# A fourth token tile read transposed, and two weight splits moved, in a linear-attention and gated-FFN kernel

## The chip, the core and the metric

The kernel runs on one core of one Trainium2 chip. The metric is the device time of one execution in microseconds; the median of three runs is given, with the lowest and the highest. One execution was also taken by the hardware profiler. The engines are named as the profile names them: PE (TensorE matmuls), PEld (TensorE weight loads), DVE (VectorE), ACT (ScalarE), POOL (GpSimd) and SP (SyncE, which issues all DMAs here).

## The reference

x has 2048 tokens of 576 features. It is layer-normalized once; the normalized x feeds a linear attention (32 heads of 18) and a feed-forward network of width 4608, whose output gates that of the attention.

```python
def _A_ref(x, wqkv, wo):                       # linear attention
    q, k, v = ...(x @ wqkv)                    # 32 heads of 18
    phi = lambda t: jnp.where(t > 0, t + 1, jnp.exp(t)) + 1e-6
    pq, pk = phi(q), phi(k)
    kv = jnp.einsum("bhsd,bhse->bhde", pk, v)
    z = jnp.einsum("bhsd->bhd", pk)
    num = jnp.einsum("bhqd,bhde->bhqe", pq, kv)
    den = jnp.einsum("bhqd,bhd->bhq", pq, z)[..., None] + 1e-6
    return (num / den ...) @ wo

def _B_ref(x, w1, b1, w2, b2):                 # feed-forward
    h = _gelu(jnp.einsum("bsd,df->bsf", x, w1) + b1)
    return jnp.einsum("bsf,fd->bsd", h, w2) + b2

xn = _layernorm(x, axis=-1)
s = _A_ref(xn, A_wqkv, A_wo)
g = _silu(_B_ref(xn, B_w1, B_b1, B_w2, B_b2))
return x + s * g
```

## The kernel before, in words

All arrays are float32. A matmul takes float32r operands, so each operand is split into a high part (a cast on ACT) and a low part (the difference, mostly on DVE), and a product is the sum of high by high, high by low and low by high. The work has three stages.

**Stage 1, keys and values** (the loop at line 539, one pass for each of 16 token tiles of 128). In pass t, TensorE projects tile t to keys (`pk`, 28 matmuls at line 313), adds the state product of tile t-1 (`ps_kva`, `ps_kvb`, line 382) and projects tile t to values (`pv`, line 313). The projection needs the normalized x of the tile transposed, features on partitions, as `xh` and `xl`. There are two ways to it, and `NTR` (line 41) says how many tiles take the first:

- tiles below NTR: x comes in rows (`load_x`); `statistics` (lines 187 to 196: bn_stats on DVE, a power on POOL) gives mean and reciprocal deviation; `normalize_x` (ACT, line 221, with `offset` on DVE before it) normalizes; `transpose_x` makes five transposes on TensorE (line 232) and takes the result out of PSUM into `xh` (ACT, line 238) and `xl` (DVE, lines 246 and 247).
- tiles from NTR on: x comes already transposed from a second input xT (`load_xt`, line 255). There the mean and deviation of each token lie along the free dimension, so `store_stats` (line 260) writes the two numbers of each token to DRAM and `load_stats` (line 264) reads them back into all 128 partitions (`bc`). `center` (POOL, line 276) subtracts, `scale` (DVE, line 279) multiplies, `set_x_hi` (ACT, line 287) and `set_x_lo` (DVE, lines 291 and 292) split. TensorE does nothing for them.

In pass t the code makes tile t+1 ready. Between these steps the pass prepares operands of the feed-forward weights: `w2_load`, `w2_sum` (POOL, 405), `w2_hi`, `w2_lo`, `w2_store` (`w2r`, `w2o`), and `we_load`, `we_sums` (POOL, 440), `we_hi` (ACT, 446), `we_lo` (DVE, 450), `we_store` (`w1u`, `w1h`). The tiles `xt` (which `xn` shares) and `bc` have three buffers each; the `xh` and `xl` of tiles 12 to 15 take the place of `w1h` and `w1u`.

**Stage 2, queries and attention** (the loop at line 1070).

**Stage 3, feed-forward** (the loop at line 1512). 18 steps: 9 chunks of four 128-wide feature blocks, for two halves of the tokens. In a step, two pairs of blocks (j = 0 and 1) go through `Up.step` seven times each (`UP`, line 1454): products at line 1148 into the banks `a`, `b`, `zy` and `e`, which DVE combines (lines 1168, 1171, 1174, 1181, 1185) and ACT turns into gelu values `g` (line 1156). Bank `e` is written twice by a pair: by step 5, whose result DVE reads at line 1174, and by step 3, which adds to what stands there. Then come seven products with w2 (`product`, line 1287). The last step is plain: it has no such products; the four blocks of w2 are split at `set_hi` (813) and `set_lo` (816) as `w__11202`, `w__11213`, `w__11226` and `w__11301`, and `down_plain` (line 1403) multiplies with them.

What each step does beside the products stands in a table written by hand: `add(base + n, fn)` puts fn behind the n-th of 28 places of a step (0 to 6 are the first pair, 7 to 13 the second), and `at_step` runs it. In stages 1 and 2 every engine, in stage 3 every engine but SP, executes in the order in which the code emits (`in_order`, line 59). DMAs are all issued by SP.

Of the kernel before, what the change touches and what calls it, by code (L numbers as in the profile page):

```python
# [22 lines left out]
NT = S // P  # L23
# [14 lines left out]
NGT = 8  # L38
NWARM = 20

NTR = 4


@with_exitstack
def linear_attention_gated_ffn(ctx, tc, x, xT, wqkv, wo, w1, w1e, b1, w2, b2, out):
# [129 lines left out]
    def load_x(t):  # L175
        xraw[t] = (
            stw.tile([P, D], F32, tag="stw", name=f"x{t}") if t < 2 else stage(D, f"x{t}")
        )
        for cs in (slice(0, HD), slice(HD, D)) if t == 0 else (slice(0, D),):
            nc.sync.dma_start(xraw[t][:, cs], x[t * P : (t + 1) * P, cs])  # L180
# [3 lines left out]
    def xt_tile(name):  # L184
        return t1.tile([P, KT * P], F32, tag="xt", name=name, bufs=3)

    def statistics(t):

        st = t1.tile([P, 2, 6], F32, tag="st", name=f"st{t}")
        nc.vector.bn_stats(st[:, 0, :], xraw[t][:, :HD])  # L190
        nc.vector.bn_stats(st[:, 1, :], xraw[t][:, HD:])
        mv = t1.tile([P, 4], F32, tag="mv", name=f"mv{t}", bufs=4)
        nc.vector.bn_aggr(mv[:, 0:2], st)
        nc.vector.tensor_scalar_add(mv[:, 2:3], mv[:, 1:2], 1e-5)
        nc.gpsimd.tensor_tensor(mv[:, 1:2], mv[:, 2:3], nhalf, op=ALU.pow)
        stats[t] = mv

    def layernorm(t):
        statistics(t)
        if t == 0:  # L200
            mv = stats[t]
            xn[t] = xt_tile(f"xn{t}")
            for dst, src in norm_parts(t):
                nc.vector.tensor_scalar(dst, src, mv[:, 0:1], mv[:, 1:2], op0=SUB, op1=MUL)
# [8 lines left out]
    def norm_parts(t):  # L213
        return (xn[t][:, :D], xraw[t]), (xn[t][:, D:], xraw[t][:, 512:])
# [40 lines left out]
    def load_xt(t):  # L255
        raw = xt_tile(f"xt{t}")
        xts[t] = raw.rearrange("p (k c) -> p k c", k=KT)
        nc.sync.dma_start(raw, xT[t])
# [5 lines left out]
    def load_stats(t):  # L264
        bcs[t] = t1.tile([P, P, 2], F32, tag="bc", name=f"bc{t}", bufs=3)
        src = st_dram[t]
        nc.sync.dma_start(
            bcs[t].rearrange("p c v -> p (c v)"),
            bass.AP(tensor=src.tensor, offset=src.offset, ap=[[0, P], [1, 2 * P]]),
        )  # L270

    def of_tokens(t, v):
        return bcs[t][:, None, :, v].to_broadcast([P, KT, P])

    def center(t):
        nc.gpsimd.tensor_tensor(xts[t], xts[t], of_tokens(t, 0), op=SUB)
# [152 lines left out]
    def we_load(q):  # L429
        if not we:  # L430
            we["u"] = x_lo(3, "w1u").rearrange("p a b -> p (a b)").bitcast(F32)
            we["h"] = x_hi(3, "w1h").rearrange("p a b -> p (a b)")
        u = we["u"][:, (q % 2) * 1024 : (q % 2) * 1024 + 1024]
        we[q] = u.rearrange("p (b c) -> p b c", b=8)
        nc.sync.dma_start(u[:, :512], w1e[q])
# [103 lines left out]
    for t in range(NT):  # L539
        for n in {0: (3, 4, 5), 1: (6, 7), 2: (8, 9)}.get(t, (t + 7,)):  # L540
            if n < NT:
                load_x(n)
        if t == 1:
            we_load(0), we_load(1)
        for n in (NTR, NTR + 1) if t == 2 else (t + 3,) if t > 2 else ():
            if n < NT:
                load_xt(n)
                load_stats(n)
        if 0 < t < NTR - 2:
            layernorm(t + 2)  # L550
        for n in {0: (), 1: (4, 5), 2: (6, 7)}.get(t, (t + 5,)):
            if n < NT:
                statistics(n)
                store_stats(n)
        if NTR <= t + 2 < NT:
            center(t + 2)
        if NTR <= t + 1 < NT:
            scale(t + 1)
        pk = bank2(f"pk{t}")
        v_t = v_bufs[t % 2]  # L560
        sums2 = W2_SUMS.get(t - 1, ())
        last = t + 1 == NT
        if t + 1 in (8, 12):
            x_block((t + 1) // 4)
        if t == 0:
            project(t, wk_h, wk_l, pk, FIRST)
            for k in range(KT):
                if k == 2:
                    offset(1)
                if k == 4:  # L570
                    normalize_x(1)
                split_w(raw_v[k], k, wv_h, wv_l, nc.vector)
            pv = bank2(f"pv{t}")
            v_cols = slice(0, 3 * G), slice(3 * G, D)
            project(t, wv_h, wv_l, pv, FIRST_V[0], cols=v_cols, end=False)
        else:
            project(t, wkv_h, wkv_l, pk, cols=(slice(0, HD), slice(HD, D + VB)))
        values = lambda: copy_v(v_t, 0, pk[:, 1, HD : HD + VB])
        if t + 1 < NTR:
            if t:  # L580
                k_t, _ = phi(t1, pk, f"k{t}", values)
            transpose_x(t + 1)
            if t == 0:
                project(t, wv_h, wv_l, pv, FIRST_V[1], cols=v_cols, begin=False)
            for j in sums2:
                w2_hi(j)
            for j in sums2:
                w2_lo(j)
            if t - 1 in WE_SUMS:
                we_hi(WE_SUMS[t - 1]), we_lo(WE_SUMS[t - 1])  # L590
            if t == 0:
                layernorm(2)
            if t + 2 < NTR:
                offset(t + 2)
            if t == 0:
                ones_columns()
                k_t, _ = phi(t1, pk, f"k{t}")
        else:
            if not last:
                set_x_hi(t + 1), set_x_lo(t + 1)  # L600
            for j in sums2:
                w2_hi(j)
            for j in sums2:
                w2_lo(j)
            if t - 1 in WE_SUMS:
                we_hi(WE_SUMS[t - 1]), we_lo(WE_SUMS[t - 1])
            k_t, _ = phi(t1, pk, f"k{t}", values)
        if pend is not None:
            if not ps_kv:
                ps_kv += [bank1("ps_kva"), bank1("ps_kvb")]  # L610
            state(*pend)
        if t == 0:
            for i, cs in enumerate(v_cols):
                copy_v(v_t, 3 * i, pv[:, i, : cs.stop - cs.start])
        else:
            pv = bank2(f"pv{t}")
            project(t, wkv_h, wkv_l, pv, cols=(slice(D + VB, 2 * D),))
            copy_v(v_t, 1, pv[:, 0, : D - VB])
        if t + 2 < NTR:
            normalize_x(t + 2)  # L620
        for j in W2_SUMS.get(t, ()):
            w2_sum(j)
        if t in WE_SUMS:
            we_sums(WE_SUMS[t])
        for k in WQ_SPLITS.get(t, ()):
            split_w(raw_q[k], k, wq_h, wq_l, nc.gpsimd if k == 0 else nc.vector)
        for k in WQ_LOADS.get(t, ()):
            raw_q[k] = load_w_raw(0, k)
        for j in W2_SUMS.get(t - 1, ()):
            w2_store(j)  # L630
        if t - 1 in WE_SUMS:
            q = WE_SUMS[t - 1]
            we_store(q)
            if q + 2 < WG:
                we_load(q + 2)
        if t in W2_LOADS:
            w2_load(W2_LOADS[t])
        if t == NT - 1:
            make_mask()
            nc.gpsimd.memset(kvz, 0.0)  # L640
        pend = (t, k_t, v_t)
# [584 lines left out]
    class HOps:  # L1226
# [6 lines left out]
        def add(self, pr, g):  # L1233
            for (par, b), t in g.items():
                self.A[pr, b, par] = t
                self.src[{(0, 0): 1, (0, 1): 2, (1, 1): 4, (1, 0): "-"}[b, par], pr] = t
# [266 lines left out]
    w2t = {}  # L1503
# [8 lines left out]
    for step in range(n_chunks):  # L1512
        half, c = divmod(step, NC)
        base = step * NS
# [36 lines left out]
        if not plain:  # L1551
            if half == 0 and c == NC - 1:
                for k, at in X_AT.items():
                    add(base + at, load_x_part, k)
                add(base + 14, lambda: x_new.update(rs=load_rests(0)))
                add(base + 25, silu_first, C11)
                for k in range(2):
                    add(base + 26 + k, combine, C12, nc.vector, slice(2 * k, 2 * k + 2))
                    add(base + 26 + k, combine, C21, nc.gpsimd, slice(2 * k, 2 * k + 2))
            for what in ("S", "hi", "lo"):  # L1560
                for (i, pr), at in PH[what].items():
                    add(base + at, getattr(h, what), i, pr)
        else:
            for f in range(CF):
                w2t[step].plain(f)
                add(base + (1, 2, 3, 8)[f], w2t[step].hi, ("p", f))
                add(base + (2, 3, 8, 9)[f], w2t[step].lo, ("p", f))
        if half == 1 and c == 0:
            add(base, silu_first, C12)
            add(base, silu_first, C21)  # L1570
# [22 lines left out]
        for j in range(CF // 2):  # L1593
            n = 2 * step + j
# [64 lines left out]
```

## Time and profile before

| | |
|---|---|
| time, median of 3 runs | 1098.45 us (1098.09 to 1099.10) |
| time of the profiled execution | 1098.02 us |
| its span, first to last instruction | 1096.3 us |
| busy: PE, PEld | 1088.6 us (99%), 1008.5 us (92%) |
| busy: DVE, ACT, POOL | 825.6 us (75%), 490.9 us (45%), 472.7 us (43%) |
| granted TensorE clock | 1.0 |
| stage 1, stage 2, stage 3 begin (chain of waits) | 1.45, 144.75, 282.61 us |
| the plain products of the last step begin (chain of waits) | 1065.28 us |

The profile's times are microseconds from the start of the span. In rows of the timeline stand start, duration, engine, line, operation, output and inputs, shapes and a count; in brackets the idle time of the engine before it and what ended it. A row of waits names who waited, for whom, the sum, the count and the longest. A chain row gives start, duration and what the time that set the end was spent on. Where a row groups several instructions (x2), its duration runs from the first one's start to the last one's end.

### The profile page before, as it was taken

Reading aid. Unit: us, or ns where it says so; the run is one execution under the profiler, and the core shown is the slowest. Engines: PE = TensorE matmul, PEld = TensorE weight load, DVE = VectorE, ACT = ScalarE, POOL = GpSimd, SP = SyncE. Lnnn points to the kernel's source line nnn. Section 1 sums busy time; section 2 is a strip of 40 time slices with the busy share of each in tenths; the row PEclk is TensorE's granted clock in tenths of the full one; section 3 lists DMA queues with packets and bytes.
Section 4 is the critical chain, followed back from the end, with each engine's and each line's share of the span. In section 5 each row is a group of like instructions: output and inputs, shape, how many; then the busy total and the mean of one; then the engine's idle time right before and its main releaser. Section 6 shows DMA issues by size and latency. Waiting matters only on the chain.

```text
span 1096.3 us, 18084 instructions
## 1 busy us (share of the span) xinstructions
PE 1088.6 (99%) x6702; PEld 1008.5 (92%) x6702; DVE 825.6 (75%) x1132; ACT 490.9 (45%) x844; POOL 472.7 (43%) x403
## 2 busy tenths in 40 slices
PE   9999999999999999999999999999999999999998
PEld 8999989999898998989989989899898998998987
DVE  7785748888798888888888888667476584664856
ACT  6454655555545354454453544524224233242352
POOL 4667444323546446464555553424234143242340
PEclk9999999999999999999999999999999999999999
DMA  7999834675959559486585779978676676766352
GB/s 248 269 262 280 311 135 160 205 242 188 342 214 344 190 211 332 152 317 233 187 330 167 287 239 405 387 249 296 210 245 217 204 236 217 229 222 228 122 181 87
DMA packets 88400, 262.54 MB, mean 239 GB/s; under 512 B 11894, under 2 KB 24182, under 8 KB 85624
## 3 DMA queue, kind: packets, MB, share of 16 engines
q1 hardware_dynamic: 88312, 261.38, 70.1%
q8 instruction: 53, 0.87, 0.3%
q14 instruction: 35, 0.29, 0.1%
HBM read 164.24 MB, written 95.17 MB: 237 GB/s over the span
## 4 chain that ended last, share of the span: by engine, by line
PE 99%; DVE 1%; issue 0%; POOL 0%; ACT 0%; DVEq 0%; POOLq 0%
PE pm L1287 35%; PE a L1148 10%; PE e L1148 10%; PE zy L1148 10%; PE pk L313 6%; PE pq L313 5%; PE ps_s L789 5%; PE b L1148 5%; PE pv L313 4%; PE pd L1403 2%; PE ps_kva L382 1%; PE ptp L771 1%; PE ps_kw L708 1%; PE warm L361 0%; PE ps_kvb L382 0%
## 5 line engine op out<-in xcount | busy, mean ns | idle before, releaser
L1293 DVE TENSOR_TENSOR macc<-pm,macc 128x576 f32<-128x576 f32 x218 | 163.8, 752 | 51.9 <-PE pm L1287 50.3
L813 ACT CAST h_h<-g 128x512 fp32r<-128x512 f32 x204 | 121.7, 621 | 133.9 <-PE pm L1287 132.8
L816 DVE TENSOR_TENSOR h_l<-g,h_h 128x512 fp32r<-128x512 f32 x204 | 161.7, 800 | 0.0
L1253 POOL TENSOR_TENSOR mid<-g 128x512 f32<-128x512 f32 x34 | 44.0, 1293 | 105.4 <-ACT g L1156 105.4
L1247 POOL TENSOR_TENSOR g<-g 128x512 f32<-128x512 f32 x34 | 54.9, 1615 | 49.4 <-DVE h_l L816 28.4
L1156 ACT ACTIVATE g<-b,b1c 128x512 f32<-128x512 f32 x36 | 24.8, 689 | 101.9 <-DVE b L1174 101.9
L1165 ACT COPY mid<-a 128x512 f32<-128x512 f32 x36 | 21.1, 585 | 96.4 <-PE a L1148 96.4
L859 POOL TENSOR_TENSOR w1raw<-w1raw 128x256 f32<-128x256 f32 x18 | 13.3, 737 | 116.7 <-ACT h_h L813 68.2
L1168 DVE TENSOR_TENSOR mid<-b,mid 128x512 f32<-128x512 f32 x36 | 24.8, 690 | 46.3 <-PE b L1148 43.0
L1375 POOL TENSOR_TENSOR fin1l<-fin1h,fin1l 128x288 f32<-128x288 f32 x8 | 6.4, 806 | 119.6 <-DMA fin1l<-s_dram 62.9
L1250 POOL TENSOR_TENSOR g<-g 128x512 f32<-128x512 f32 x34 | 55.2, 1623 | 2.7
L1148 PE MATMUL a<-h0r,wa 128*128 128x512 f32 x144 | 50.4, 390 | 0.0
L1148 PE MATMUL a<-xh,wa 128*128 128x512 f32 x144 | 50.4, 390 | 0.0
L816 DVE TENSOR_TENSOR h_l<-mid,h_h 128x512 fp32r<-128x512 f32 x34 | 48.8, 1437 | 1.2
L1156 ACT ACTIVATE g<-e,b1c 128x512 f32<-128x512 f32 x36 | 24.8, 689 | 51.5 <-DVE e L1181 51.5
L754 POOL TENSOR_TENSOR pbuf<-phiq,den 128x576 f32<-128x576 f32 x16 | 19.4, 1214 | 63.9 <-DVE den L753 63.9
L1244 POOL TENSOR_TENSOR g<-g 128x512 f32<-128x512 f32 x34 | 44.2, 1299 | 2.7
L1181 DVE TENSOR_TENSOR e<-e,mid 128x512 f32<-128x512 f32 x36 | 24.8, 689 | 21.5 <-PE e L1148 21.5
L1171 DVE TENSOR_TENSOR mid<-zy,mid 128x512 f32<-128x512 f32 x36 | 24.9, 691 | 19.5 <-PE zy L1148 19.5
L313 PE MATMUL pk<-wkv_h,xh 128*128 128x288 f32 (+1 forms) x160 | 38.1, 320 | 0.5 <-DVE xh L245 0.5
L313 PE MATMUL pk<-wkv_l,xh 128*128 128x288 f32 (+1 forms) x160 | 38.2, 321 | 0.0
L1174 DVE TENSOR_TENSOR b<-e,mid 128x512 f32<-128x512 f32 x36 | 25.2, 699 | 17.2 <-PE e L1148 16.2
(857 smaller groups left out, 3644.4 us busy)
## 6 DMA issues: line engine op xcount, KB each, us to landing
we<-we_dram SPq DMA_DIRECT2D x36, 448.0 KB
w2raw<-w SPq DMA_DIRECT2D x10, 1152.0 KB
op<-w2o SPq DMA_DIRECT2D x18, 576.0 KB
w1raw<-w SPq DMA_DIRECT2D x18, 512.0 KB
op_a<-wa SPq DMA_DIRECT2D x18, 512.0 KB
op_c<-wc SPq DMA_DIRECT2D x18, 512.0 KB
op_d<-wd SPq DMA_DIRECT2D x18, 512.0 KB
wc<-op_c SPq DMA_DIRECT2D x18, 512.0 KB
```

Of the source, the lines that this page charges most:

```text
L313: nc.tensor.matmul(ps[:, h, : ws.stop - ws.start], st, w[:, k, ws], start=(begin and i == 0), stop=(end and i == len(seq) - 1), skip_group ...
L789: nc.tensor.matmul(ps[:, h, :HD], st[:, k, :], w[:, k, h * HD : (h + 1) * HD], start=(i == 0), stop=(i == len(seq) - 1),)
L813: nc.scalar.copy(pair[0], src)
L816: eng.tensor_tensor(pair[1], src, pair[0].bitcast(F32), op=SUB)
L1148: nc.tensor.matmul(ps, st, mv, start=first and n == 0, stop=n == len(seq) - 1, skip_group_check=True,)
L1156: nc.scalar.activation(g, ps, AF.Gelu_apprx_tanh, bias=b1c[:, f : f + 1])
L1244: tt(src[5, pr], A(1, 0), A(1, 1), op=ADD)
L1247: tt(src[6, pr], src[5, pr], A(0, 0), op=SUB)
L1250: tt(src[3, pr], A(0, 1), src[6, pr], op=SUB)
L1253: tt(src[7, pr], A(0, 0), A(1, 0), op=SUB)
L1287: nc.tensor.matmul(ps[:, q, :HD], hs[p][st][:, cs], m[:, p, :], start=(n == 0 and i not in CHAIN), stop=(n == 5), skip_group_check=True,)
L1293: nc.vector.tensor_tensor(dst, src, dst, op=ADD)
```

## The change

Two things change. `NTR` goes from 4 to 3, so tile 3 takes the second way; the loads, stores, centerings and scalings of the first passes are listed anew so that tile 3 has its own: in pass 1 its xT load, the store of its statistics and, behind the stores of tiles 4 and 5, the load of its broadcast; in pass 2 its centering (ahead of tile 4's), its scaling and its split. In the last step, the high and low parts of w2's blocks 2 and 3 move from places 3/8 and 8/9 to places 3/4 and 4/5.

```diff
-NTR = 4
+NTR = 3
...
         if t == 1:
             we_load(0), we_load(1)
-        for n in (NTR, NTR + 1) if t == 2 else (t + 3,) if t > 2 else ():
+        for n in {0: (), 1: (), 2: (4, 5)}.get(t, (t + 3,)):
             if n < NT:
                 load_xt(n)
                 load_stats(n)
-        if 0 < t < NTR - 2:
-            layernorm(t + 2)
-        for n in {0: (), 1: (4, 5), 2: (6, 7)}.get(t, (t + 5,)):
+        if t == 1:
+            load_xt(NTR)
+        for n in {0: (), 1: (3, 4, 5), 2: (6, 7)}.get(t, (t + 5,)):
             if n < NT:
                 statistics(n)
                 store_stats(n)
-        if NTR <= t + 2 < NT:
-            center(t + 2)
+        if t == 1:
+            load_stats(NTR)
+        for n in {0: (), 1: (), 2: (3, 4)}.get(t, (t + 2,)):
+            if n < NT:
+                center(n)
         if NTR <= t + 1 < NT:
             scale(t + 1)
...
         else:
             for f in range(CF):
                 w2t[step].plain(f)
-                add(base + (1, 2, 3, 8)[f], w2t[step].hi, ("p", f))
-                add(base + (2, 3, 8, 9)[f], w2t[step].lo, ("p", f))
+                add(base + (1, 2, 3, 4)[f], w2t[step].hi, ("p", f))
+                add(base + (2, 3, 4, 5)[f], w2t[step].lo, ("p", f))
```

The rest of a pass follows from `NTR`: `transpose_x`, `offset` and `normalize_x` are called for tiles below it, `set_x_hi` and `set_x_lo` for the others.

## The prediction

> **What bounds the kernel now.** I read the page first, its engine totals and the chain that ended last, then TensorE's waits over the whole span.
>
> ```profile
> PE 1088.6 (99%) x6702; PEld 1008.5 (92%) x6702; DVE 825.6 (75%) x1132; ACT 490.9 (45%) x844; POOL 472.7 (43%) x403
> ...
> PE 99%; DVE 1%; issue 0%; POOL 0%; ACT 0%; DVEq 0%; POOLq 0%
> ```
>
> ```profile
> PE warm L361 <- POOL ident masks.py:199: 1.5, 1, 1.5
> PE pk L313 <- DVE xh L245: 0.5, 1, 0.5
> PE e L1148 <- DVE b L1174: 0.3, 1, 0.3
> ```
>
> TensorE (PE) is busy for 1088.6 of 1096.3 us, the chain is 99% TensorE, and after its first instructions TensorE waits for another engine twice: 0.5 us at the start, which the change does not reach, and 0.3 us at line 1148. So the time is the sum of TensorE's work. An edit can make the kernel faster in two ways only: by taking TensorE instructions away, or by removing that 0.3 us. It makes it slower wherever it creates a wait of TensorE. The change does both good things, in small amounts, and adds one chain of work that could create a wait.
>
> **Part 1a: five transposes go.** Tile 3 no longer passes through `transpose_x`. What this is worth is read from the chain in the pass of token tile 2, where these transposes stand (start, us, what), and from two windows, the pass of tile 2 and that of tile 3, which has no transposes (start to end, length, busy time of PE, PEld, DVE, ACT, POOL).
>
> ```profile
> 25.94 4.48 PE pk L313 x28
> 30.42 0.55 PE pt L232 x5
> 30.96 0.89 PE ps_kva L382 x8
> ```
>
> ```profile
> 25.78:34.78 9.00, 9.00 (x58) 8.71 (x57) 3.89 (x12) 5.28 (x10) 1.28 (x3) 1.00 0.78 239
> 34.78:43.23 8.45, 8.45 (x53) 8.21 (x52) 6.95 (x10) 4.49 (x9) 7.54 (x5) 1.00 0.94 227
> ```
>
> The five transposes hold 0.55 us of the chain, and the pass with them takes 9.00 us against 8.45 without: both readings give **-0.55 us**. The granted clock is 1.00 in both.
>
> **Part 1b: what takes their place, and whether it is in time.** Tile 3 now needs xT loaded (128 x 640 x 4 bytes, 320 KB), its statistics stored and read back as a broadcast (bc, 128 x 256 x 4, 128 KB), a centering on POOL, a scaling and a low part on DVE, a high part on ACT. Its statistics stay where they were on DVE. Gone are its normalization on ACT (1.21 us in line 221), the offset and the copies out of PSUM. The rows that price and place these:
>
> ```profile
> 34.58 0.39 PEld L313 LDWEIGHTS pk<-wkv_h,xh 128*128 128x128 f32 x2
> 35.23 0.37 PEld L313 LDWEIGHTS pk<-wkv_h,xl 128*128 128x128 f32 x2
> 35.61 1.60 POOL L276 TENSOR_TENSOR xt<-xt,bc 128x640 f32<-128x640 f32 x1 [7.00 <-DMA bc<-st_dram]
> 39.30 0.72 ACT L287 CAST xh<-xt 128x640 fp32r<-128x640 f32 x1 [3.73 <-DVE xt L279]
> 40.06 1.03 DVE L291 TENSOR_TENSOR xl<-xt,xh 128x512 fp32r<-128x512 f32 x1 [0.79 <-ACT xh L287]
> 46.18 0.83 DVE L279 TENSOR_TENSOR xt<-xt,bc 128x640 f32<-128x640 f32 x1
> 26.46 1.21 ACT L221 ACTIVATE xn<-x,mv 128x576 f32<-128x576 f32 x2
> 28.05 0.55 POOL L195 TENSOR_TENSOR mv<-mv,nhalf 128x1 f32<-128x1 f32 x1 [0.74 <-DVE mv L194]
> 30.46 0.65 ACT L326 ACTIVATE ek<-pk 128x576 f32<-128x576 f32 x1 [2.79 <-PE pk L313]
> 32.69 0.76 DVE L332 SCALAR_TENSOR_TENSOR phik<-pk,ek 128x576 f32<-128x576 f32 x1 [4.71 <-ACT ek L330]
> ```
>
> The deadline: the projection of tile 3 loads its first xh as weights at 34.58 and its first xl at 35.23; with 0.55 us less ahead of it these become 34.03 and 34.68. The start: on POOL the centering of tile 3 stands behind the power of tile 7, which ends at 28.60. From there: centering 1.60 to 30.20, scaling 0.83 to 31.08 (with 0.05 to pass the signal on), high part 0.72 to 31.85, low part 1.03 to 32.91. Margin: 2.2 us for xh, 1.8 us for xl. The cover is idle time that the rows show: POOL idle 7.00 us before 35.61, DVE 4.71 before 32.69, ACT 2.79 before 30.46. On ACT the phi of tile 2 (line 326) now queues behind the high part and ends up some 2 us later; its end was 33.45, and its result is first read by the state product behind the projection of tile 3 (34.58 and some 4.5 us), at 39, so nothing on TensorE waits. I cost all this at **0**; if the cover is gone, it is the wait worked out below.
>
> The one duration that the trace doesn't have is the landing of tile 3's broadcast. SP's queue and three windows (the last two columns are DMA share and GB/s):
>
> ```profile
> 24.18 0.33 SPq L262 DMA_DIRECT2D st_dram<-mv  x1
> 24.55 0.42 SPq L394 DMA_DIRECT2D w2r<-w  x1
> 25.07 2.42 SPq L180 DMA_DIRECT2D x<-x  x2
> ...
> 28.33 1.43 SPq L267 DMA_DIRECT2D bc<-st_dram  x1
> ```
>
> ```profile
> 15.00:20.00 5.00, 5.00 (x35) 5.00 (x34) 3.87 (x10) 3.36 (x8) 1.49 (x4) 1.00 1.04 403
> 20.00:25.00 5.00, 4.96 (x34) 4.50 (x33) 4.63 (x15) 4.10 (x10) 2.92 (x8) 1.00 0.16 41
> 25.00:30.00 5.00, 5.00 (x32) 4.93 (x31) 2.61 (x10) 1.69 (x4) 1.98 (x4) 1.00 0.70 60
> ```
>
> The new load is issued behind the store of tile 5 (24.18) and ahead of w2r, at about 24.55, so to 25.05. Bound from below: it lands at once. From above: tile 4's broadcast, issued by 29.76 with 864 KB of w2r, two x tiles and an xT tile in front of it, had landed by 35.61, 5.9 us later; so 30.9. In front of tile 3's broadcast stands only a 1 KB store, and the engines were 16% busy in the 5 us before, so it lies near the lower end: I take it landed before 28.60, which costs nothing. Without any collision the wait of TensorE is the landing minus 30.37 (34.68 less 4.31 for the rest of the chain), 0.5 us at the upper bound.
>
> The xT load stands at the end of what fills the queue until about 20 us; at the 403 GB/s of that stage its 320 KB take 0.8 us, in the idle stretch from 20 to 25. SP itself gains: the two x issues at 25.07 take 2.42 us where one takes about 0.4, since the second waits for the buffer of tile 3's x until its normalization has read it; that wait of some 1.5 us goes. What moves behind the new broadcast (w2r, two x tiles, tile 4's xT and broadcast) moves by 128 KB, 0.3 us.
>
> Behind tile 3, every tile up to 15 must be ready 0.55 us sooner. The tightest is tile 12, whose xh buffer is that of w1h and must wait for w1h's store:
>
> ```profile
> 109.02 0.73 ACT L287 CAST xh<-xt 128x640 fp32r<-128x640 f32 x1 [5.87 <-DMA we_dram<-w1h]
> ```
>
> ```profile
> 110.60 0.39 PEld L313 LDWEIGHTS pk<-wkv_h,xh 128*128 128x128 f32 x2
> ```
>
> It ends at 109.75, 0.85 us before TensorE loads it at 110.60. After the change 0.30 us are left if the store does not move with TensorE. Cost 0, with that cover.
>
> **Part 2: the last chunk.** The high and low parts of w2's blocks 2 and 3 move from the second pair's steps to the first pair's. DVE and TensorE around it:
>
> ```profile
> 1051.98 0.70 DVE L1181 TENSOR_TENSOR e<-e,mid 128x512 f32<-128x512 f32 x1 [1.74 <-PE e L1148]
> 1053.57 0.70 DVE L1185 TENSOR_TENSOR zy<-zy,mid 128x512 f32<-128x512 f32 x1 [0.89 <-PE zy L1148]
> 1056.80 0.69 DVE L1168 TENSOR_TENSOR mid<-b,mid 128x512 f32<-128x512 f32 x1 [2.53 <-PE b L1148]
> 1057.40 1.27 DVE L816 TENSOR_TENSOR w__11226<-w2raw,w__11226 128x576 fp32r<-128x576 f32 x1
> ...
> 1059.80 0.74 DVE L816 TENSOR_TENSOR w__11301<-w2raw,w__11301 128x576 fp32r<-128x576 f32 x1
> ...
> 1061.07 0.69 DVE L1174 TENSOR_TENSOR b<-e,mid 128x512 f32<-128x512 f32 x1
> ```
>
> ```profile
> 1050.35 1.59 PE e L1148 x7
> ...
> 1061.81 1.89 PE e L1148 x7
> ```
>
> TensorE writes bank e again at 1061.81 only after DVE's line 1174 has read it. That read comes at 1061.07 because 1.27 + 0.74 us of the two w2 splits stand before it. With them gone it starts when the products of e end: line 1168 starts at the end of b's, 1056.8, zy's and e's take 1.59 each, so 1060.0; it ends at 1060.7, 0.8 us before TensorE would come (1061.81 - 0.30). The group's place in the chain falls from 1.89 to 1.59: **-0.30 us**. In the first pair the two splits meet DVE idle for 1.74 and 0.89 us: line 1181 may come 0.1 to 0.5 us later, line 1185 up to 0.6; TensorE writes these banks again at the earliest with the second pair's e, at 1058.4, over 5 us behind line 1181. Cost 0.
>
> **Sum:** -0.55 - 0.30 = -0.85 us. Against the profiled execution, 1098.02 us (span 1096.3 and 1.7 around it): 1097.17. That execution lies 0.43 below the median of the runs, 1098.45; against the median I forecast **1097.6**.
>
> **The rivals.**
>
> *Tile 3's broadcast lands late (slower).* Place: POOL line 276 for tile 3. Nothing is gained in the end from a landing at 31.2 on, where the wait reaches 0.85 us. The far price comes from the longest readings of the same instructions:
>
> ```profile
> 37.24 2.03 DVE L279 TENSOR_TENSOR xt<-xt,bc 128x640 f32<-128x640 f32 x1 [0.58 <-POOL xt L276]
> ...
> 41.47 2.19 POOL L276 TENSOR_TENSOR xt<-xt,bc 128x640 f32<-128x640 f32 x1
> ...
> 47.80 1.70 DVE L291 TENSOR_TENSOR xl<-xt,xh 128x512 fp32r<-128x512 f32 x1 [0.79 <-ACT xh L287]
> ```
>
> 2.19, 2.03 and 1.70 in place of 1.60, 0.83 and 1.03 add 2.46 us; from a landing at 30.9 the wait is 0.5 + 2.46 = 3.0 us, so 1098.45 - 0.85 + 3.0 = 1100.6. For it: the DMA engines moved only 60 GB/s from 25 to 30 us at a share of 0.70, so something is slow there. Against: the place in the queue.
>
> *POOL and DVE collide at tile 3.* If tile 4's centering starts before tile 3's scaling, the scaling takes 2.03 and the low part 1.70, 1.87 us more, against a margin of 1.8: 1097.7. Against it: tile 4's broadcast landed at 35.6. The Trainium skill, SBUF — State Buffer, section "SBUF: two separate sides", states a harder rule: a DVE operation with two inputs in SBUF and a GpSimd operation share a port pair as an exclusive lock, and the second waits for the whole of the first. The 2.03 us row, which ran beside a POOL operation, fits a lock more than free passage. By the rule each of the two DVE operations waits up to one centering (1.60 us), 3.2 in all, 1.4 beyond the margin: an estimate of 1099.0.
>
> *Tile 12's store lands later than the cover.* A wait of up to 0.85 us takes back what was gained: 1097.6 to 1098.4.
>
> *The wait at line 1148 stays*, since other splits reach DVE before 1174: 1097.9.
>
> **How the numbers follow.** Forecast 0.59; tile 12 0.13; line 1148 stays 0.06; collision 0.06; late broadcast 0.10; a gain or a loss of over 2.2 us that I don't see 0.03 each. The three runs of before lie from 0.36 under to 0.65 over their median; so the forecast's own spread is 1097.2 to 1098.3, and tile 12 and the collision reach 1099.0. The range, 1096.6 to 1099.3, leaves out the two unseen cases and the greater part of the late broadcast, 0.13 in all. A measurement of this kernel tells about 0.2% (2.2 us) from no change; of the cases only the far end of the late broadcast (0.04 of its 0.10: a landing near 30.9 with all three long readings) and the unseen loss pass it upward, only the unseen gain downward: faster 0.03, same 0.90, slower 0.07.
>
> **What would show it.** Right: no transposes of pt behind tile 2, the pass of tile 2 at 8.45 us, POOL's line 276 beginning near 28.5, no wait of PE pk on ACT xh or DVE xl; the e group of the last chunk at 1.59 and no PE wait on line 1174. Wrong: a wait of pk L313 for xh L287 or xl L291 at 34 or at 110 us, a centering of tile 3 released by the DMA of bc after 30.4, or new waits past 144 us.

## The result, and the profile after

The changed kernel took 1101.74 us (median of 7 runs, 1099.95 to 1103.73) against 1098.45 us before (7 runs, 1097.63 to 1099.10): ratio 1.0033, 95% interval 1.0023 to 1.0043. The forecast was 1097.6 us, the range ended at 1099.3: **the change makes the kernel slower by about 3.3 us**. The profiled execution took 1103.73 us, the longest of the seven, with a span of 1102.0 us. The page's totals and its chain first, then TensorE's four longest waits (who, for whom, sum, count, longest); the line numbers behind the first edit are three higher than before.

```profile
PE 1089.6 (99%) x6697; PEld 1008.4 (92%) x6697; DVE 831.7 (75%) x1132; ACT 489.8 (44%) x842; POOL 476.1 (43%) x404
...
PE 96%; DVE 1%; issue 1%; ACT 1%; DMA 1%; SPq 0%; POOL 0%; DVEq 0%; ACTq 0%
```

```profile
PE pk L313 <- ACT xh L287: 2.6, 1, 2.6
PE warm L361 <- POOL ident masks.py:199: 1.4, 1, 1.4
PE e L1151 <- DVE b L1177: 1.3, 1, 1.3
PE a L1151 <- ACT mid L1168: 1.0, 1, 1.0
```

TensorE has five instructions fewer and is yet busy 1.0 us longer, and two of these waits are new: 2.6 us at the keys of tile 3 and 1.0 us at bank a. The wait at bank e was to go; at 1.3 us it is four times as long as before (0.3).

**Where it goes, in stage 1.** The chain that ended last, in tile 3 (start, us, what):

```profile
26.08 4.49 PE pk L313 x28
30.57 3.31 issue
33.88 1.57 POOL xt L276
...
35.48 0.83 DVE xt L279
...
36.34 0.73 ACT xh L287
...
37.11 6.42 PE pk L313 x28
```

The transposes are gone, and behind the keys of tile 2 the chain leaves TensorE. POOL's centering starts at 33.88, long after the power of tile 7, and then centering, scaling and high part follow without a gap. The keys of tile 3 start at 37.11; before it was 34.78. They then take 6.42 us for the 28 matmuls that took 4.47. Two windows of before, then two of after (start to end, length, busy time of the engines, clock, DMA share, GB/s), and a third of after:

```profile
29.00:31.00 2.00, 2.00 (x16) 1.95 (x15) 0.00 (x0) 0.54 (x1) 0.00 (x0) 1.00 0.62 235
31.00:33.00 2.00, 2.00 (x16) 1.91 (x15) 0.31 (x1) 1.97 (x5) 0.00 (x0) 1.00 1.01 402
```

```profile
29.00:31.00 2.00, 2.00 (x16) 1.99 (x15) 0.00 (x0) 0.00 (x0) 0.00 (x0) 1.00 0.72 23
31.00:33.00 2.00, 2.00 (x14) 1.87 (x14) 0.00 (x0) 0.00 (x0) 0.00 (x0) 1.00 0.97 154
39.00:41.00 2.00, 2.00 (x8) 1.96 (x8) 1.20 (x3) 1.44 (x4) 2.00 (x2) 0.50 0.54 201
```

From 29 to 31 us the DMA engines are 72% busy and move 23 GB/s; before, 62% moved 235. And from 39 to 41 us, behind TensorE's wait, the granted clock is 0.50, with 8 matmuls where the windows at full clock have 14 to 16. So tile 3 costs twice: 2.7 us of wait and 1.8 us of slow clock (from the first matmul of the keys to the first of the state product 6.26 us, 4.47 before), against 0.55 us gained. SP had issued the broadcast early:

```profile
25.05 0.32 SPq L267 DMA_DIRECT2D bc<-st_dram  x1
```

The trace names no releaser for the centering, but it has a record of each packet of this load: 128 packets of 1024 bytes, of which the last ends at 33.46, 8.4 us after the issue began and 0.4 us before the centering starts. So the centering waited for the broadcast; why the broadcast is slow is tried below.

**In the last step.** DVE's low parts of w2 and POOL's combines of `macc`, after, then the same lines before:

```profile
1051.98 0.90 DVE L819 TENSOR_TENSOR w__11200<-w2raw,w__11200 128x576 fp32r<-128x576 f32 x1
1053.57 3.23 DVE L819 TENSOR_TENSOR w__11211<-w2raw,w__11211 128x576 fp32r<-128x576 f32 x1
1056.72 3.23 DVE L819 TENSOR_TENSOR w__11224<-w2raw,w__11224 128x576 fp32r<-128x576 f32 x1
1060.47 2.64 DVE L819 TENSOR_TENSOR w__11236<-w2raw,w__11236 128x576 fp32r<-128x576 f32 x1
```

```profile
1053.50 9.00 POOL L1306 TENSOR_TENSOR macc<-macc 128x1152 f32<-128x1152 f32 x3
```

```profile
1049.48 0.76 DVE L816 TENSOR_TENSOR w__11213<-w2raw,w__11213 128x576 fp32r<-128x576 f32 x1
```

```profile
1049.58 8.47 POOL L1303 TENSOR_TENSOR macc<-macc 128x1152 f32<-128x1152 f32 x3
```

Before, the second low part started 0.10 us ahead of POOL's three combines and took 0.76 us; the third began 0.65 us before their end and took 1.27 us, and the fourth came behind them (0.74). After, the second starts 0.07 us behind the first combine and takes 3.23 us, and the moved third and fourth stand beside the other two combines. Line 1188 (1185 in the kernel before), in which DVE combines bank zy, has to wait behind the fourth low part, ACT's gelu waits for line 1188, ACT's copy out of bank a comes behind the gelu, and TensorE waits for the copy before it can write bank a again. Counted from the beginning of the step, TensorE is 1.2 us later when it writes bank a for the second time in the second pair, and 2.2 us later from bank e on.

Sum by the starts of TensorE's groups: 0.13 from the first microseconds, -0.54 for the transposes, 2.74 of wait and 1.79 of clock make 4.12 behind tile 3, and 4.16 when the last step begins. The last step adds 2.2. The plain products start at 1071.65, 6.37 us later than before (1065.28), and so does DVE's last product. What follows that takes 0.67 us less, which I did not follow up, so the span is 5.7 us longer.

### The profile page after: what moved, and what is told of

Read it like the earlier page. It is cut to its first block, busy times and chain, and to the rows that moved or that the text cites. A ratio compares the mean times of both kernels' runs of the same rounds, so it can differ in the third digit from the quotient of the medians.

```text
span 1102.0 us, 18080 instructions
## 1 busy us (share of the span) xinstructions
PE 1089.6 (99%) x6697; PEld 1008.4 (92%) x6697; DVE 831.7 (75%) x1132; ACT 489.8 (44%) x842; POOL 476.1 (43%) x404
## 4 chain that ended last, share of the span: by engine, by line
PE 96%; DVE 1%; issue 1%; ACT 1%; DMA 1%; SPq 0%; POOL 0%; DVEq 0%; ACTq 0%
PE pm L1290 35%; PE e L1151 10%; PE zy L1151 10%; PE a L1151 10%; PE pk L313 6%; PE pq L313 5%; PE ps_s L792 5%; PE b L1151 5%; PE pv L313 4%; PE pd L1406 2%; PE ps_kva L382 1%; PE ptp L774 1%; PE ps_kw L711 1%; DMA raw_v<-wqkv 1%; DVE w__11224 L819 0%
## 5 line engine op out<-in xcount | busy, mean ns | idle before, releaser
L862 POOL TENSOR_TENSOR w1raw<-w1raw 128x256 f32<-128x256 f32 x18 | 13.3, 737 | 116.9 <-ACT h_h L816 68.2
```

## Experiments

They ran on other chips than the first comparison; there the kernel before scatters more (1097.9 to 1106.2 us). The expectations name their theories afresh each time. The text names the kernel from which each diff is made.

### Each part alone

`t3_alone` has only the `NTR` part, `tail_alone` only the two `add` lines; their diffs are those parts of the change.

> The first part of the change alone (tile 3 read transposed, the w2 splits where they were). Theory: the broadcast of tile 3's statistics lands late, near 33 us, TensorE waits some 2 to 3 us before the projection of tile 3 and then runs at half the granted clock for about 3 us (1.8 us more); with the five transposes gone (-0.55) the kernel is 2 to 4 us slower than before, 1100.5 to 1102.5, and the last chunk looks as before (one wait of 0.3 at bank e). Rival: the wait at tile 3 comes from a rare landing and the median is within 1 us of before, so that most of the 3.3 us of the change comes from the last chunk.

> The second part alone (w2's blocks 2 and 3 split in the first pair's steps, four tiles by transposes). Theory: the low parts meet the three combine operations that POOL runs one after the other from about 1049.6, each holding DVE up for nearly its whole length of about 3 us; splits of 2.6 to 3.2 us in place of 0.75, TensorE waits 1 us for bank a and 1.3 us for bank e, 1.5 to 2 us slower than before (1100 to 1100.5), and stage 1 as before. Rival: the collision came about only because the first part had moved POOL against DVE; then the splits take 0.75 to 1.3 us as before and the kernel is 0.3 us faster (1098.1).

`t3_alone`: 1103.50 us, ratio 1.0029 (1.0013 to 1.0046). Its profiled execution (1109.59 us) waits 3.1 us at tile 3 and pays 2.8 us of clock behind it, and then waits again at tile 12, 4.7 and 2.1. `tail_alone`: 1100.11 us, ratio 1.0001 (0.9986 to 1.0017). Its second low part and its combines:

```profile
1054.30 0.75 DVE L816 TENSOR_TENSOR w__11213<-w2raw,w__11213 128x576 fp32r<-128x576 f32 x1
```

```profile
1054.40 9.53 POOL L1303 TENSOR_TENSOR macc<-macc 128x1152 f32<-128x1152 f32 x3
```

Here DVE's second low part started 0.10 us ahead of POOL; the third and fourth still took 2.52 and 2.63 us, but nothing on TensorE waited for them, the 0.3 us at bank e was gone, and the second pair's last zy came 0.2 us sooner in the step than before. So the first part carries a loss of its own; the second has the same collision, but in these two profiles whether it cost anything went with 0.1 us in the start of one low part.

### Who goes first, DVE or POOL

`tail_comb4` is `tail_alone` with each combine in four pieces; `tail_combdve` has the combines on DVE; `after_again` is the kernel after once more; `after_comb4` is it with the four pieces.

```diff
-                add(base + 4, combine, m, nc.gpsimd)
+                for q in range(QH):
+                    add(base + 4, combine, m, nc.gpsimd, slice(q, q + 1))
...
-            for m in (C12, C21, C22):
-                add(base + 4, combine, m, nc.gpsimd)
+            for m, at in ((C12, 0), (C21, 0), (C22, 3)):
+                add(base + at, combine, m, nc.vector)
```

> As the second part alone, but POOL's three combine operations cut into four pieces each (one per token tile), the same work in pieces of about 0.75 us. Theory (an exclusive hold for the length of one POOL instruction): each low part waits at most one piece, so 0.75 to 1.5 us, the waits of TensorE at banks a and e go, about 1098.1. Rival (the two engines share a port and slow each other in proportion, whatever the length): the splits stay at 2.6 to 3.2 us and the time stays that of the second part alone, about 1100.3.

> The unchanged kernel after, profiled and timed once more. Tile 3: theory A expects again a wait of 2.4 to 4.5 us at its key matmuls and 1.7 to 2.8 us of slow clock behind it. Last chunk: if who goes first on the port is decided by about 0.1 us, the second low part of w2 on VectorE takes either about 0.75 us (it starts ahead of GpSimd's first combine, no wait at bank e) or 3.2 us (it starts behind it, a wait of 1 us or more at banks a and e). The rival, that the tail loss is fixed, expects 3.2 us and both waits again. Time 1100 to 1104 us; ratio to the kernel before 1.002 to 1.005.

> The kernel after, with GpSimd's three combines each cut into four pieces of 288 columns. If a combine holds VectorE off for the whole of one instruction, the low parts of w2 fall to at most 1.5 us each, the waits at banks a and e go, and banks e to zy come 0.3 to 0.5 us earlier than in the kernel before; tile 3 stays as in the kernel after (a wait of 2.4 to 4.5 us and 1.7 to 2.8 us of slow clock). If tile 3 carries the loss, the ratio to the kernel before stays at 1.001 to 1.004, no more than 0.002 under that of the kernel after on the same chip; if the last chunk carries it, it falls to 1.000 or below.

> Only the w2 part of the change, with the three combines moved from GpSimd to VectorE (two of them ahead of the second half of the step, one behind it). If the port between the two engines is what holds the low parts, they take 0.74 to 1.3 us each with no GpSimd instruction beside them, and no wait comes at banks a and e; VectorE has three instructions of about 1.3 us each more, which fit into its idle time in these steps. Ratio to the kernel before 0.998 to 1.001. If the low parts are long for another reason (the transfers of w2, say), they stay at 2.5 us or more.

The low parts in `after_comb4`:

```profile
1052.64 0.96 DVE L819 TENSOR_TENSOR w__11200<-w2raw,w__11200 128x576 fp32r<-128x576 f32 x1
1054.23 0.75 DVE L819 TENSOR_TENSOR w__11211<-w2raw,w__11211 128x576 fp32r<-128x576 f32 x1
1055.64 1.39 DVE L819 TENSOR_TENSOR w__11224<-w2raw,w__11224 128x576 fp32r<-128x576 f32 x1 [0.66 <-ACT w__11224 L816]
1057.55 0.76 DVE L819 TENSOR_TENSOR w__11236<-w2raw,w__11236 128x576 fp32r<-128x576 f32 x1
```

With quarter-length combines no low part takes over 1.4 us; with no combine on POOL at all (`tail_combdve`) they take 0.74 to 0.75 each. In both, and in `tail_comb4` (1.12, 0.76, 1.41, 0.77), no wait is left at banks a and e, and TensorE reaches the second pair's last zy 0.6 us sooner than before. `after_again` repeats the collision (3.09, 3.22, 2.62 us, waits of 0.8 at a and 1.3 at e), so with whole combines and the moved splits POOL came first in two profiles of three. The times: `after_again` 1103.54 us, ratio 1.0027 (1.0013 to 1.0041); `after_comb4` 1101.81 us, 1.0012 (0.9995 to 1.0029); `tail_comb4` 1098.72 us, 0.9988 (0.9974 to 1.0003); `tail_combdve` 1099.78 us, 1.0004 (0.9989 to 1.0019). By medians, cutting the combines takes 1.7 us off the kernel after and leaves 2.0 us of loss; by ratio the loss left is 1.3 us, with an interval from -0.5 to 3.2 that reaches no loss at all. The profile of `after_comb4` puts what is left at tile 3 (2.9 us of wait, 1.7 of clock). That POOL's combines hold the low parts is shown: the low parts shrink when the combines are shortened, and the hold is gone when no combine runs on POOL. The lengths fit a hold for about one whole combine. (On DVE a combine took 1.7 to 2.0 us, more than I had expected.)

### Tile 3: the place in the queue

`t3_early` is `t3_alone` with tile 3's broadcast issued right behind its own store, ahead of the stores of tiles 4 and 5.

```diff
                 store_stats(n)
-        if t == 1:
-            load_stats(NTR)
+                if n == NTR:
+                    load_stats(n)
```

> As the first part alone, but tile 3's broadcast is issued right behind its own store, ahead of the stores of tiles 4 and 5. Theory A (the reads are slow for some microseconds after each store in pieces of 8 bytes, so what counts is how many such stores are ahead): the broadcast has one store ahead in place of three and lands by 26 to 27; centering right behind the power of tile 7 at 28.5, no wait of TensorE at tile 3, 0.5 us faster than before, 1097.9. Theory B (the slow stretch from 25 to 33 us is there for another reason, whatever is ahead): the broadcast is out at about 23 and either slips through before 25, or lands as late as in the first part alone; the store of tile 4 is held up on SP until tile 3's has landed, about 1 us.

1105.59 us, ratio 1.0048 (1.0034 to 1.0063). POOL's centerings of tiles 3 and 4:

```profile
29.37 1.59 POOL L276 TENSOR_TENSOR xt<-xt,bc 128x640 f32<-128x640 f32 x1 [0.66 <-issue]
40.86 1.59 POOL L276 TENSOR_TENSOR xt<-xt,bc 128x640 f32<-128x640 f32 x1 [9.90 <-DMA bc<-st_dram]
```

Tile 3 is in time, as I had wanted it. But tile 4's broadcast now comes behind the two later stores and is late, with 2.3 us of wait and 2.1 of clock, and tile 12 waits 3.7 us with 1.7 of clock behind it. The wait went to the next broadcast behind a cluster of stores.

### Tile 3: the stores, and the clock

`t3_double` is `t3_alone` with each store of statistics made twice; `t3_warm` is it with 24 transposes of the identity into `pk` ahead of tile 3's keys (their result is overwritten), so that TensorE is busy while it would wait.

```diff
-        nc.sync.dma_start(st_dram[t], stats.pop(t)[:, :2])
+        nc.sync.dma_start(st_dram[t], stats[t][:, :2])
+        again = dram.tile([P, 2], F32, name=f"st_again{t}")
+        nc.sync.dma_start(again, stats.pop(t)[:, :2])
...
+            if t == NTR:
+                for _ in range(24):
+                    nc.tensor.transpose(pk[:, 0, :P], ident, ident)
```

> As the first part alone, but every store of statistics is made twice, to another place in DRAM. Theory A: twice as many 8-byte pieces make the slow stretch longer; tile 3's broadcast lands later than 34 us, say 37 to 40, and the wait at tile 3 grows from 2.7-3.1 to 5 or more. Theory B: three more issues of 0.33 us on SP ahead of the broadcast, 1 us later, and nothing else.

> As the first part alone, with 24 extra transposes of the identity (0.11 us each, 2.6 us) on TensorE ahead of the projection of tile 3, in the bank that the projection then overwrites; they fill the wait with work whose result is thrown away. Theory (the granted clock falls to 0.50 after a wait of 2.6 us or more, and this costs 1.8 to 2.8 us behind the wait): the projection of tile 3 takes 4.5 us in place of 6.4 to 7.2, the clock is 1.00 from 34 to 45 us, and the kernel is about 2 us faster than the first part alone. Rival (the slow projection is the wait for xl and the contended memory): it still takes 6 us or more, and the clock falls all the same.

`t3_double`, one execution: 1112.02 us; the wait at tile 3 grows to 6.4 us, and tile 12 waits 4.1. The issue of the broadcast begins only 0.2 us later than in `t3_alone` (25.38 and 25.17), but its last packet ends 3.6 us later (37.50 and 33.93). So more stores make the read behind them later, and not by their time in SP's queue. `t3_warm`: 1105.28 us, ratio 1.0053 (1.0039 to 1.0068, 4 runs). Its windows at tile 3:

```profile
34.00:37.00 3.00, 3.00 (x24) 2.83 (x23) 0.00 (x0) 0.00 (x0) 1.52 (x1) 1.00 0.98 359
37.00:41.00 4.00, 3.40 (x25) 3.06 (x24) 2.90 (x4) 3.02 (x6) 0.05 (x1) 1.00 0.87 314
```

The clock stays at 1.00, and the keys take 4.67 us from first start to the next group's, where they took 6.26 in the kernel after and 7.23 in `t3_alone`, from which it is changed: the slow clock comes from TensorE's idle time and costs 1.6 to 2.8 us by itself in these profiles. The Trainium skill, TensorE: Matmul & The Clock Gate, section "Part 1: The HAM clock gate", lets the clock halve after one idle window of some 3.4 us; here it halved behind a wait of 2.57 us in the kernel after and, in this profile at tile 12, behind one of 1.9 us (0.52 from 117 to 119 us), so the measured waits are the safer bound. The time of the whole kernel gained nothing: TensorE was busy, the broadcast as late as ever, this profile also waits at tile 12 (1.9 us, and 1.7 of clock), and it lost 1.1 us to a late first load. Why its ratio lies above that of `t3_alone` stays open.

### Statistics stored in rows

If the stores are to blame, other stores must help. In `t3_wide` (from `t3_alone`) and `b4_wide` (from `before`) DVE turns the statistics by 32 x 32 blocks, so that a store is 8 pieces of 128 bytes and not 128 of 8; the broadcast reads the same 128 rows of 1 KB, with the means ahead of the deviations. In `t3_wide2` (from `after_comb4`) and `b4_wide2` (from `tail_comb4`) the turn and store of tiles from 6 on stand behind DVE's `scale` of the same pass, where it has one, and in `t3_wide2` those of tiles 4 and 5 behind tile 2's transposes, with tile 3's broadcast ahead of them.

```diff
-        st_dram[t] = dram.tile([P, 2], F32, name=f"st_dram{t}")
-        nc.sync.dma_start(st_dram[t], stats.pop(t)[:, :2])
+        rows = t1.tile([P, 32], F32, tag="mvt", name=f"mvt{t}", bufs=2)
+        nc.vector.transpose(rows, stats.pop(t))
+        st_dram[t] = dram.tile([2, 4, 32], F32, name=f"st_dram{t}")
+        for v in range(2):
+            nc.sync.dma_start(st_dram[t][v], rows[v : v + 97 : 32, :])
...
         if NTR <= t + 1 < NT:
             scale(t + 1)
+        for n in {0: (), 1: (), 2: (6, 7)}.get(t, (t + 5,)):
+            if n < NT:
+                store_stats(n)
```

> As the first part alone, but the statistics of a tile are turned by a 32x32 transpose on DVE before they are stored, so that a store is 8 pieces of 128 bytes in place of 128 pieces of 8 bytes (two issues of 4 pieces each), and the broadcast holds the means in front of the deviations. Theory A (reads by DMA are slow for 4 to 6 us after a store in 8-byte pieces): the slow stretch at 25 to 33 us goes, tile 3's broadcast lands by 27, no wait of TensorE at tile 3, 4 or 12, granted clock 1.00 throughout, 1097.9 or less, 0.5 us under an undisturbed run of before. Theory B (the stretch comes from something else at that time): the wait of 2.7 to 3.1 us at tile 3 stays and the time stays near 1103.

> The kernel before (four tiles by transposes) with the same wide stores. Theory A: as before in its undisturbed runs, 1098.2, but without the runs of 1100 to 1105, since the wait at tile 12 goes as well; t3_wide is 0.55 us faster than this one, the five transposes. Theory B: the median and the spread of before stay.

> The kernel after with its combines cut in four, and the statistics stored in rows: VectorE turns them by 32 x 32 blocks, so that a store is 8 pieces of 128 bytes and not 128 of 8. Unlike the earlier kernel with such stores, only tile 3's turn and store stand ahead in the pass of tile 1 (4 and 5 behind the transposes of tile 2), and from tile 3 on the turns stand behind VectorE's multiply, so that it doesn't wait for GpSimd there. Theory A (reads behind many 8-byte stores are slow, and that alone makes tile 3 late) expects the wait at tile 3 under 0.6 us, its key matmuls at 4.5 to 4.7 us and 4.47 us from tile 5 on, tile 3's key matmuls no more than 0.3 us behind the kernel before's, and 1097 to 1098.5 us, ratio 0.997 to 1.000. Theory B (the row broadcast is late for its place in SyncE's queue, whatever the stores look like) expects a wait of 1.5 us or more at tile 3 or 4 with slow clock behind it, and 1100 us or more.

> The kernel before (four tiles transposed on TensorE) with the w2 splits moved, the combines cut in four and the statistics stored in rows as in t3_wide2, the turns behind VectorE's multiply. Theory A (slow reads behind 8-byte stores also make tile 12 late, and the 0.45 us that each tile lost in the earlier kernel with row stores was VectorE waiting for GpSimd's power ahead of its multiply) expects 4.47 us for the key matmuls of each tile from 5 on, no wait at tile 12, and 1097 to 1098.5 us in nearly all runs, ratio 0.996 to 0.999. If the 0.45 us came from the stores or the other layout of the broadcast, each tile from 4 to 11 still takes 4.85 us or more, and the ratio stays at 1.001 or above; if tile 12's wait has another cause, some runs lie at 1101 us or above.

The slow stretch is gone with the 8-byte stores. A window of before, just behind the stores, where SP issues the load of `w2r` at 24.55, and two of `b4_wide`, where it issues the same load at 26.32:

```profile
25.00:27.00 2.00, 2.00 (x13) 1.93 (x12) 1.90 (x8) 1.02 (x3) 1.12 (x3) 1.00 1.05 28
```

```profile
27.00:29.00 2.00, 2.00 (x14) 2.00 (x13) 1.68 (x8) 1.02 (x2) 0.82 (x2) 1.00 0.74 162
29.00:31.00 2.00, 2.00 (x15) 1.95 (x15) 0.21 (x1) 0.19 (x1) 0.28 (x1) 1.00 0.99 396
```

The times do not show it yet. `t3_wide`: 1105.09 us, ratio 1.0050 (1.0036 to 1.0064); `b4_wide`: 1101.49 us, 1.0015 (1.0003 to 1.0026). The wait at tile 12 was gone in both and that at tile 3 down to 0.2 us in `t3_wide`; but there DVE's turns ahead of tile 2's work made tile 2 late by 1.1 us and tile 4 waited 1.3, and in both kernels the keys of each tile from 5 to 11 took 0.4 to 0.5 us longer. DVE in `b4_wide` shows why:

```profile
58.17 0.21 DVE L264 STREAM_TRANSPOSE mvt<-mvb 128x32 f32<-128x32 f32 x1 [0.66 <-POOL mvb L197]
58.31 2.04 DVE L284 TENSOR_TENSOR xt<-xt,bc 128x640 f32<-128x640 f32 x1
61.14 0.91 DVE L296 TENSOR_TENSOR xl<-xt,xh 128x512 fp32r<-128x512 f32 x1 [0.80 <-ACT xh L292]
```

The turn waits for POOL's power, the scaling behind it then runs beside POOL's centering (2.04 us, not 0.83), and the low part arrives while TensorE is already in its keys. With the turn behind the scaling, in `b4_wide2`:

```profile
63.18 0.83 DVE L284 TENSOR_TENSOR xt<-xt,bc 128x640 f32<-128x640 f32 x1
64.45 0.21 DVE L264 STREAM_TRANSPOSE mvt<-mvb 128x32 f32<-128x32 f32 x1 [0.44 <-POOL mvb L197]
```

`b4_wide2`: 1097.39 us (12 runs, 1097.00 to 1098.61), ratio 0.9968 (0.9957 to 0.9979); `t3_wide2`: 1097.73 us (12 runs, 1097.22 to 1098.89), ratio 0.9974 (0.9961 to 0.9987). **Both beat the kernel before** that ran beside them, and the scatter is gone; the kernel after did not run beside them, but its ratios to the kernel before (1.0033 and 1.0027) lie above 1. In its profile `b4_wide2` gains in the last step, the 0.6 us of `tail_comb4`; its stage 1 takes as long as in an undisturbed profile of the kernel before (110.45 us from tile 2 to tile 15, and 110.36). So the rest of its ratio must come from runs of the kernel before that waited in stage 1 (their median was 1100 us and not 1098), which neither of that kernel's two profiles shows. In `t3_wide2`, SP's issue of tile 3's broadcast, POOL's centering of it, and the waits of TensorE that are left, but for that of the warm-up:

```profile
27.57 0.33 SPq L272 DMA_DIRECT2D bc<-st_dram  x1
```

```profile
30.73 0.55 POOL L197 TENSOR_TENSOR mvb<-mvb,nhalf 128x1 f32<-128x1 f32 x1 [0.61 <-DVE mvb L196]
31.25 1.56 POOL L281 TENSOR_TENSOR xt<-xt,bc 128x640 f32<-128x640 f32 x1
```

```profile
PE pt0a L234 <- DVE xn L206: 1.2, 1, 1.2
PE pk L318 <- DVE xh L247: 0.6, 1, 0.6
PE pt L234 <- ACT xn L223: 0.3, 1, 0.3
PE pk L318 <- DVE xl L296: 0.2, 1, 0.2
```

The broadcast is issued 2.5 us later than in the kernel after, and the centering starts right behind POOL's powers. But this kernel changes two things, since only one store stands ahead of the broadcast here. The packet records part them (128 packets of 1024 bytes each; us):

| kernel | stores of statistics ahead | issue begins | last packet ends | from one to the other | median packet |
|---|---|---|---|---|---|
| kernel after | three, 8-byte pieces | 25.05 | 33.46 | 8.4 | 0.30 |
| `t3_alone` | three, 8-byte pieces | 25.17 | 33.93 | 8.8 | 0.31 |
| `t3_double` | six, 8-byte pieces | 25.38 | 37.50 | 12.1 | 0.36 |
| `t3_early` | one, 8-byte pieces | 24.76 | 28.90 | 4.1 | 0.17 |
| `t3_wide` | three, 128-byte pieces | 27.97 | 32.67 | 4.7 | 0.07 |
| `t3_wide2` | one, 128-byte pieces | 27.57 | 30.14 | 2.6 | 0.05 |

With the same number of stores ahead, larger pieces take the broadcast from 8.4 to 4.7 us, or from 4.1 to 2.6; with the same pieces, fewer stores ahead help too. Both count. Tile 3's keys follow those of tile 2 by 8.45 us, without a wait: the 0.55 us is there. But tile 4's keys take 4.94 us, 0.47 more, since its broadcast takes 5.35 us to land and its low part is late: the gain is given back one tile on, and `t3_wide2` is no faster than `b4_wide2`, which still has the transposes. This profile (1098.86 us) is also the second longest of the twelve runs, with a clock of 0.50 from 10 to 12 us behind waits of 1.2 and 0.6 us close together.

### The wait at tile 12 in the kernel before

> The unchanged kernel before, profiled once more, on another chip than its first profile. Theory A (a late row broadcast, then a lowered clock, are nothing that only the change brings; tile 12 has little cover in every kernel) expects no wait at tile 3, 4.48 us for each tile's key matmuls up to tile 11, and either no wait at tile 12 (about 1098 us) or one of 2.7 to 3 us with 1.75 us of slow clock behind it (about 1102.5 us). The rival, that the wait at tile 12 comes from the edited kernels alone, expects none, and 1098 us. In the last chunk both expect low parts of w2 in under 1.3 us each and a wait of 0.3 us at bank e.

1098.96 us; no wait at tile 3, 0.3 us at tile 12, 0.4 at bank e. So the kernel before was undisturbed in both of its profiles, but three kernels whose stage 1 is its own were not. The chain of `tail_alone` there:

```profile
104.09 8.94 DMA we_dram<-w1h
...
113.13 0.73 ACT xh L287
...
113.91 6.19 PE pk L313 x27
```

TensorE waits 2.8 us for the store of `w1h`, whose buffer `xh` takes, and then pays 1.75 us of clock (the keys take 6.22 us, not 4.47); `tail_comb4` (2.5 us) and `tail_combdve` (2.0) have it too. With row stores no run of `b4_wide2` lies above 1098.61, while the 23 runs of the kernel before beside it reach 1104.46. That the 8-byte stores make this store late too is what fits, but no run changes it alone. SP issues the last 8-byte store at 101.58, 2.5 us ahead of it. The traces show two delays. In `tail_alone` the store is issued at 104.09 and not at 101.19 as in before, behind a centering for which the broadcast came 2.9 us later. And in the ten profiles where an 8-byte store is issued 1.3 to 2.9 us ahead of it, the cast that waits for it starts 7.8 to 13.3 us after its issue; in the kernel after, where that store is 5.8 us ahead, and in the two `b4_wide` kernels it is 4.7 us.

## Why the prediction was wrong, point by point

- **The transposes, -0.55: right** (0.54 in the kernel after, 0.55 in `t3_wide2`).
- **The step that failed first: "I take it landed before 28.60, which costs nothing."** The broadcast's last packet ended at 33.46, TensorE waited 2.74 us and then lost 1.79 to the clock. The landing was bounded from above by tile 4's broadcast, 5.9 us after its issue, and even that bound was too low: tile 4's ran partly behind the slow stretch, tile 3's stood in the middle of it. The window that the prediction quotes had the sign: 25 to 30 us at a share of 0.70 and 60 GB/s. I wrote that "something is slow there", and set the place in the queue against it; and I counted only the last store ahead, by its 1 KB. Three stores of 128 pieces each stood there. `t3_early` shows that the broadcast is quick with one of them ahead, `t3_double` that it is slower with six, and the row stores that the size of the pieces counts. The rival *Tile 3's broadcast lands late* was the right mechanism with a chance of 0.10. Its price of 3.0 us came from another sum (long readings of POOL and DVE, which did not occur: 1.57, 0.83, 0.69), and happened to lie near the 2.7 us of wait: luck. A time clear of noise on the slow side had been given a chance of 0.07.
- **A term that was missing: the clock.** 1.8 us behind the wait were in no rival. The late broadcast should have been priced at wait plus slow clock, near 4.5 us.
- **"The two splits meet DVE idle ... Cost 0": wrong.** The idle time was there, but I read DVE's rows and bank e, not POOL's. The three combines stood in the trace of before at 1049.58, with the second low part 0.10 us ahead of them. The rule that I weighed at tile 3 (the Trainium skill, SBUF — State Buffer, section "SBUF: two separate sides": a shared port pair held for a whole instruction) holds here: 3.23 us against 0.75 alone, 1.4 with pieces of a quarter. The contended price that the trace offered, about 1.3 us, was too small by half, since a combine is long. In the last step of the kernel after, the collision made TensorE 2.2 us later. The -0.30 at bank e was right where DVE isn't held: `tail_comb4`, `tail_combdve` and `after_comb4` have it and more.
- **SP's gain of 1.5 us: wrong.** The two x issues took 3.41 us, more than the 2.42 before.
- **The rival at tile 12** was priced at 0.85 us and put down to the change. It is a wait of up to 2.8 us with the stage 1 of before (4.7 in `t3_alone`), with a slow clock behind it, and it comes without the change too.
- **The collision at tile 3** did not come (DVE scaling 0.83). *Line 1148 stays* was right for the kernel after, by another way.

How the medians share out: tile 3 alone costs 3.2 us by ratio (1.4 to 5.1), tile 3 with the last step repaired 1.3 (-0.5 to 3.2), the last step alone 0.1 (-1.5 to 1.9). The intervals overlap; the single terms rest on the profiles, not on these ratios.

## What to carry to other kernels

When TensorE is busy for 99% of the span, a gain of half a microsecond is lost to the first wait, and behind the waits of 1.9 us and more here the clock cost another 1.6 to 2.8 us: price both. For a load that the trace doesn't show, look at what the queue is writing ahead of it: here a share near 1 with few GB/s (1.05 and 28 GB/s in the kernel before) went with small pieces under way. A place ahead of them handed the delay to the next read; larger pieces took it away. Before you move a DVE instruction with two inputs in SBUF into idle time, read POOL's rows there; cutting the long POOL instruction into pieces ended the hold here.

## What the hardware showed that I had not expected

- Stores of 128 pieces of 8 bytes slow the reads behind them: from 29 to 31 us 23 GB/s at a share of 0.72 behind three such stores, 235 GB/s at 0.62 behind two. Behind those two, from 25 to 27 us, it was 28 GB/s at 1.05. With stores in pieces of 128 bytes a broadcast landed 4.7 us after its issue behind three stores, and 2.6 behind one, instead of 8.4 and 4.1.
- The clock fell to 0.50 behind a wait of 2.57 us and cost 1.8 us; the shortest single wait whose price was measured was 1.9 us (1.7 of clock). Kept busy, TensorE ran at 1.00.
- Which of two engines starts first was decided by 0.07 to 0.2 us, and with whole combines it was worth 2.4 us (2.2 us later in the kernel after, 0.2 sooner in `tail_alone`).
